# From batch 1 on, x is turned by VectorE block transposes and a trip through DRAM instead of by TensorE

## The chip, the cores and the metric

The program runs on one core of one Trainium2 chip. The time is the device time of one execution in microseconds (us), the median of three runs. Four engines compute: TensorE (PE in the profile; its weight loads are PEld), VectorE (DVE), ScalarE (ACT) and GpSimd (POOL). SyncE (SP) issues all DMAs of this kernel, one after the other in its own program order. Every engine works through its instructions in order, so an instruction that waits holds up all that stand behind it on the same engine.

## The reference

Two stages, in float32, for 8 batches of 576 tokens and 512 channels (8 heads of 64). Attention, of which half the heads see a window of 32 and half a dilated window:

```python
scores = scale * np.matmul(q, k.transpose(0, 1, 3, 2))
scores = np.where(masks[None, :, :, :], scores, -1000000000.0)
attn = softmax over the last axis          # max, exp, sum, divide
x = np.matmul(attn, v), heads side by side # (B, S, 512)
```

and then a mixing stage on its result x:

```python
theta = x @ w_theta
zr, zi = x * np.cos(theta), x * np.sin(theta)
y = einsum('ts,bsd->btd', w_tok_r, zr) + einsum('ts,bsd->btd', w_tok_i, zi)
u = x + y
return u + np.maximum(u @ w_ch, 0.0)
```

## The kernel before

Attention leaves x channel-major: four tiles `xf[b, c]` (c = 0 to 3) with 128 channels on the partitions and 576 tokens along the row. Theta comes out of TensorE the other way, with tokens on the partitions: five tiles, st = 4 (64 tokens) and then st = 0, 1, 2, 3 (128 tokens each), 512 channels along the row. For the products x·cos and x·sin x is therefore needed token-major too. `natural` makes it: for each st, four TensorE transposes (`nc.tensor.transpose` against the identity `idt`, L718) write a 128x512 tile `xn` in PSUM, which the two products read from there.

The work of one tile st after its theta is the trig stage. ScalarE converts theta/2π to an integer (`K`, L746), VectorE takes the fraction (L748), ScalarE makes the sine (`g`, L754), the absolute value (L695) and the cosine (L697), VectorE multiplies by x (L760 sine, L702 cosine; L767 and L702 for the tile of 64), ScalarE rounds the product to `zh` (L641) and GpSimd subtracts to get the rest `zl` (L643). Tiles `K` and `g` have two buffers each.

From batch 1 on the program is a sequence of phases (`phase(b, nb)`), written out in a fixed order. A phase runs the mixing stage of batch b on TensorE while it makes x and z of batch nb = b+1 and begins the attention of batch b+2:

- Eight token units (`token`, L804: 27 matmuls each into a bank `y`), each followed by a residual on VectorE (L782). Between them stand the scores of nb's pairs 2 and 3 and of the next batch's pairs 0 and 1 (L465), and the products with v (`pv`, L614, bank `o`) for the four pairs of nb.
- Scores go through a softmax: the mask and maximum on VectorE (L406, L495), the exponential on ScalarE (L501), the sum's inverse on VectorE (L504, L505), the scaling on GpSimd (L507), and eight 32-row block transposes on VectorE (`turn`, L522) that give `pt`, which `pv` reads.
- After each `pv` ScalarE copies the bank to `x` (L578) and rounds it to `xh` (L590); VectorE subtracts for pairs 0 to 2 (L594, L596), GpSimd for pair 3.
- Then five thetas alternate with channel units (`chan`, L834, 12 matmuls into a bank `c`), each unit followed by a VectorE finish (L813); the `xn` transposes stand in TensorE's order between a channel unit and the next theta. Three channel units close the phase.

Token and channel units share two PSUM banks (tag `m`), so a unit starts only when the residual or finish of the unit two places before it is done. TensorE keeps the order of the code. What VectorE, ScalarE, GpSimd and SP do in a phase is put in order by a scheduler when the program is built. The part up to the end of batch 0 (about the first 142 us) is ordered by `Order` instead, a planner that takes ranks and estimated costs (such as `yield "DVE", 1000`); here the x and z of batch 1 are made. Phases b = 1 to 5 have the same order of VectorE and ScalarE before the change; phase 6 begins no further attention, and phase 7 only mixes.

The changed lines and the functions around them:

Of the kernel before, what the change touches and what calls it, by code (L numbers as in the profile page):

```python
# [48 lines left out]
TURN_AT = {2: 0, 3: 1, 4: 5}  # L49
TURN_TH = {5: 1}  # L50
TH_AT = 7
NK = 9


# [5 lines left out]
class Order:  # L60
# [84 lines left out]
def dma(n):  # L145
    return 128 * 4 * n / 360.0
# [3 lines left out]
def build(ctx, tc, qT, kT, vw, wth, wtk, wch, maskb, ident, identb, outT):  # L150
# [3 lines left out]
    sp = ctx.enter_context(tc.tile_pool(name="soft", bufs=2))  # L154
    xp = ctx.enter_context(tc.tile_pool(name="xu", bufs=2))
    hp = ctx.enter_context(tc.tile_pool(name="hilo", bufs=1))
    gp = ctx.enter_context(tc.tile_pool(name="trig", bufs=2))
    ps_s = ctx.enter_context(tc.tile_pool(name="ps_s", bufs=2, space=PSUM))
    ps_v = ctx.enter_context(tc.tile_pool(name="ps_v", bufs=1, space=PSUM))
# [36 lines left out]
    def give(tag, n):  # L196
        if od.live:
            signal(("free", tag, n))
# [401 lines left out]
    def pv(b, pr):  # L600
        yield None, ("va", b, pr)
        yield None, ("vb", b, pr)
        yield None, ("pt", b, pr)
        if pr >= 1:
            yield None, ("pv", b, pr - 1)
        (va, ra), (vb, rb) = vs["a", b, pr], vs["b", b, pr]
        xf[b, pr] = xp.tile([128, S], F32, tag=f"x{pr}", name=f"x{b}_{pr}")
        n = yield from take("v", 1)
        ps = ps_v.tile([128, 2 * DM], F32, tag="v", name=f"o{b}_{pr}")[:, :S]
        yield "PE", 1300  # L610
        for j in range(NJ):
            v = va[:, j] if j < VA else vb[:, j - VA]
            for hh in range(2):
                pe(nc.tensor.matmul(ps[64 * hh:64 * hh + 64, BW * j:BW * j + BW], v[:, 64 * hh:64 * hh + 64],  # L614
                                    pmats[b, pr][:, j, hh], start=True, stop=True))
        go(x_evac(b, pr, ps, ("v", n), ("xe", b, pr)))
        signal(("pv", b, pr))
        n = b * NP + pr
        if ra is not None:
            give("va", ra)  # L620
            go(load_va(n + 2), RANK["load"])
        if rb is not None:
            give("vb", rb)
            go(load_vb(NP if n == NP - 2 else n + 1), RANK["load"])
        if b:
            go(x_split(b, pr))

    zs = {}

# [63 lines left out]
    def cosine(b, st, f, z, kt, key, rel):  # L693
        yield "ACT", act(DM)
        pin(nc.scalar.activation(f, f, AF.Abs))  # L695
        yield "ACT", act(DM) + 90
        table(nc.scalar.activation(f, f, AF.Sin, scale=-2 * math.pi, bias=halfpi[:f.shape[0]]))  # L697
        signal(("sin", b, st))
        yield None, ("xn", b, st)
        px, rx = pxs[b, st]  # L700
        yield "DVE", dve(DM)
        pin(nc.vector.tensor_tensor(z, px, f, op=ALU.mult))  # L702
        signal(key)
        if kt is not None:
            yield None, ("px", b, st)
            give(*rx)
            yield from zsplit(b, kt, z, rel)
        elif rel:
            give(*rel)

    pxs = {}

    def natural(b, st, cs):
        px, rx = yield from bank("mmxxm"[st] if b == 0 else "x" if b == 1 else XP[st], f"xn{b}_{st}")
        px = px[:cs.stop - cs.start]
        yield "PE", 430
        for c in range(NC):
            pe(nc.tensor.transpose(px[:, 128 * c:128 * c + 128], xf[b, c][:, cs], idt))  # L718
        pxs[b, st] = px, rx
        signal(("xn", b, st))  # L720

    def trig(b, st):
        cs = slice(128 * st, min(128 * st + 128, S))
        R = cs.stop - cs.start
        yield None, ("th", b, st) if b else ("th0", st, 3)
        pt, rt = ths.pop((b, st))
        go(natural(b, st, cs))
        if b == 0 and st in FG0:
            K, gt = (hp.tile([128, DM], F32R, tag=t, name=f"{n}{b}_{st}").bitcast(F32) for t, n in zip(FG0[st], "Kg"))
            K = K.bitcast(I32)[:R]  # L730
            rf = rg = None
        else:
            rf, rg = ("f", (yield from take("f", 2))), ("g", (yield from take("g", 2)))
            K = gp.tile([128, DM], I32, tag="f", name=f"K{b}_{st}")[:R]
            gt = gp.tile([128, DM], F32, tag="g", name=f"g{b}_{st}")
        f = K.bitcast(F32)
        g = gt[:R]
        th = pt[:R]
        if R == 64 and b > 0:
            yield "ACT", act(DM)  # L740
            pin(nc.scalar.copy(g, pt[R:]))
            yield "DVE", dve(DM)
            pin(nc.vector.tensor_tensor(g, th, g, op=ALU.add))
# [10 lines left out]
        table(nc.scalar.activation(g, f, AF.Sin, scale=2 * math.pi))  # L754
        if R == 128:
            go(cosine(b, st, f, f, st, ("cos", b, st), rf))
            yield None, ("xn", b, st)
            px, rx = pxs[b, st]
            yield "DVE", dve(DM)
            pin(nc.vector.tensor_tensor(g, px, g, op=ALU.mult))  # L760
            signal(("px", b, st))
            yield from zsplit(b, 4 + st, g, rg)
        else:
            yield None, ("xn", b, st)
            px, rx = pxs[b, st]
            yield "DVE", dve(DM)
            pin(nc.vector.tensor_tensor(gt[128 - R:], px, g, op=ALU.mult))  # L767
            yield from cosine(b, st, f, g, None, ("cos", b, st), rf)
            give(*rx)
            yield from zsplit(b, 8, gt, rg)  # L770

    uh, ul = {}, {}
# [68 lines left out]
    def phase(b, nb):  # L841
# [5 lines left out]
        while n <= TH_AT:  # L847
            for p in S_AT:
                if S_AT[p] == n and nb + p // NP < B:
                    go(scores(nb + p // NP, p % NP))  # L850
            f, i, g = UNITS[n]
            go(f(b, i, g))
            for p in range(NP):
                if PV_AT[p] == n:
                    go(pv(nb, p))
            for p in TURN_AT:
                if TURN_AT[p] == n and nb + p // NP < B:
                    go(turn(nb + p // NP, p % NP))
            n += 1
        rest = UNITS[n:]  # L860
        for i, st in enumerate(STS):
# [65 lines left out]
    for p in range(2):  # L927
        go(scores(2, p), RANK["scores2"] + p * RANK["pair"])
        go(turn(2, p), RANK["scores2"] + p * RANK["pair"])
    go(thetas(1), RANK["theta1"])  # L930
    od.run()
    od.live = False
# [70 lines left out]
```

## Time and profile before

| | |
|---|---|
| median of three runs | 597.24 us (596.74 to 597.54) |
| the profiled execution | 597.07 us, of which the span from first to last instruction is 595.3 us |
| mean granted TensorE clock | 0.984 |
| busy time in the span | PE 569.7, PEld 516.9, DVE 361.6, ACT 351.1, POOL 222.4 us |
| moved by DMA | 67.76 MB, 114 GB/s on average |

The profile page gives busy times of the engines, the chain of work that ended last, and groups of equal instructions; the trace behind it can be asked for stretches of time, waits, and instructions in order of time. A row of the timeline has the start and the duration in us, the engine, the line, the operation, the tiles (out<-in) and, in brackets, how long the engine stood idle before it and what ended that. A row of the chain of waits has start, duration, engine, tile, line, and how many instructions are merged in it.

### The profile page before, as it was taken

The page shows a single profiled execution, that of the slowest core. Times are in us where ns is not written, and L with a number is a line of the kernel's source. Part 1 is how long each engine was busy: PE and PEld are TensorE (multiplying, and loading weights), DVE is VectorE, ACT ScalarE, POOL GpSimd, SP SyncE. Part 2 cuts the span into 40 slices and gives each one's busy share as a digit, 9 for nine tenths or more (in the row PEclk, how much of TensorE's full clock was granted, in tenths as well). Part 3 has the DMA queues.
Part 4 walks back from the last instruction along what each step waited for, and adds up shares of the span by engine and source line. Part 5 has one row for each costly group of instructions (what it writes and reads, how often), then busy time and mean ns, then how long its engine had stood idle before and what let it go on. Part 6 is the DMA issues. An engine that isn't in the chain of part 4 may idle for free.

```text
span 595.3 us, 14176 instructions
## 1 busy us (share of the span) xinstructions
PE 569.7 (96%) x5584; PEld 516.9 (87%) x5584; DVE 361.6 (61%) x1132; ACT 351.1 (59%) x939; POOL 222.4 (37%) x206
## 2 busy tenths in 40 slices
PE   5997898999999999999999999999999999999997
PEld 4744787979998899889998899989998899989997
DVE  3889888855765667465566567655665656445112
ACT  1498967687535955568553974468564785266110
POOL 2229854534322532326142442316324253315220
PEclk9999599999999999999999999999999999999999
DMA  8982347404650074302641054401742023001002
GB/s 303 398 339 61 121 160 246 142 1 141 182 160 3 2 241 142 101 2 89 197 139 62 1 181 151 154 1 40 231 142 73 0 81 100 1 1 53 28 1 81
DMA packets 26866, 67.76 MB, mean 114 GB/s; under 512 B 2992, under 2 KB 3248, under 8 KB 26800
## 3 DMA queue, kind: packets, MB, share of 16 engines
q1 hardware_dynamic: 26800, 66.86, 32.9%
q8 instruction: 44, 0.72, 0.5%
q14 instruction: 22, 0.18, 0.1%
HBM read 57.41 MB, written 9.44 MB: 112 GB/s over the span
## 4 chain that ended last, share of the span: by engine, by line
PE 49%; DVE 22%; ACT 21%; issue 3%; POOL 2%; DMA 2%; SPq 0%; ACTq 0%; DVEq 0%; POOLq 0%
PE y L804 27%; DVE pt L522 9%; PE c L834 8%; PE s L465 5%; ACT P L501 5%; PE o L614 4%; PE th L682 3%; ACT K L697 3%; ACT zh L641 3%; ACT g L754 2%; ACT K L695 2%; DVE P L406 2%; DVE K L702 2%; POOL P L507 2%; ACT L754 1%
## 5 line engine op out<-in xcount | busy, mean ns | idle before, releaser
L787 POOL TENSOR_TENSOR u<-x,u 128x288 fp32r<-128x288 f32 x64 | 54.9, 858 | 184.9 <-ACT u L785 162.2
L522 DVE STREAM_TRANSPOSE pt<-P 32x288 f32<-32x288 f32 x224 | 105.1, 469 | 21.1 <-POOL P L507 18.0
L834 PE MATMUL c<-u,late_wc 128*128 128x288 f32 x768 | 111.7, 296 | 0.8 <-DVE x L813 0.5
L834 PEld LDWEIGHTS c<-u,late_wc 128*128 128x128 f32 x768 | 106.2, 188 | 4.8 <-DVE x L813 2.0
L785 ACT CAST u<-x 128x288 fp32r<-128x288 f32 x64 | 27.5, 430 | 129.3 <-DVE x L782 129.3
L804 PE MATMUL y<-wtkh,zh 128*128 128x288 f32 x288 | 90.6, 315 | 1.1 <-ACT zh L641 1.1
L804 PE MATMUL y<-wtkh,zl 128*128 128x288 f32 x288 | 86.6, 301 | 3.7 <-POOL zl L643 3.7
L804 PE MATMUL y<-wtkl,zh 128*128 128x288 f32 x288 | 86.2, 299 | 0.0
L643 POOL TENSOR_TENSOR zl<-g,zh 128x512 fp32r<-128x512 f32 x40 | 52.6, 1316 | 79.1 <-ACT zh L641 66.7
L501 ACT ACTIVATE P<-P,mx 128x64 f32<-128x64 f32 x216 | 72.1, 336 | 16.8 <-DVE mx L495 16.8
L682 PE MATMUL th<-wthh,xh 128*128 128x512 f32 x224 | 76.3, 402 | 0.0
L782 DVE TENSOR_TENSOR x<-y,x 128x288 f32<-128x288 f32 x64 | 28.7, 450 | 66.8 <-PE y L804 64.0
L804 PE MATMUL y<-late_wt_b,zh 128*128 128x288 f32 x320 | 68.1, 297 | 0.0
L804 PE MATMUL y<-late_wt_a,zh 128*128 128x288 f32 x256 | 58.0, 308 | 2.7 <-DVE x L782 2.7
L804 PEld LDWEIGHTS y<-wtkh,zh 128*128 128x128 f32 x288 | 55.4, 192 | 4.8 <-ACT zh L641 2.3
L804 PEld LDWEIGHTS y<-wtkh,zl 128*128 128x128 f32 x288 | 55.3, 192 | 4.5 <-POOL zl L643 4.5
L804 PEld LDWEIGHTS y<-wtkl,zh 128*128 128x128 f32 x288 | 55.5, 193 | 0.3 <-issue 0.3
L643 POOL TENSOR_TENSOR zl<-K,zh 128x512 fp32r<-128x512 f32 x32 | 42.0, 1312 | 36.1 <-ACT zh L641 36.1
L507 POOL TENSOR_TENSOR P<-P,sm 128x576 f32<-128x576 f32 x32 | 37.5, 1172 | 43.8 <-ACT xh L590 19.3
L804 PEld LDWEIGHTS y<-late_wt_b,zh 128*128 128x128 f32 x320 | 51.4, 189 | 0.3
L682 PEld LDWEIGHTS th<-wthh,xh 128*128 128x128 f32 x224 | 42.1, 188 | 8.3
L804 PE MATMUL y<-late_wt_b,zl 128*128 128x288 f32 x160 | 47.3, 296 | 0.0
(103 smaller groups left out, 1110.0 us busy)
## 6 DMA issues: line engine op xcount, KB each, us to landing
q<-in_qT_dram SPq DMA_DIRECT2D x32, 576.0 KB, 4.2
va<-in_vw_dram SPq DMA_DIRECT2D x30, 320.0 KB, 3.2
out_dram<-x SPq DMA_DIRECT2D x32, 288.0 KB, 2.1
k<-in_kT_dram SPq DMA_DIRECT2D x28, 304.0 KB, 4.6
vb<-in_vw_dram SPq DMA_DIRECT2D x29, 256.0 KB, 3.4
st_wtk<-in_wtk_dram SPq DMA_DIRECT2D x8, 576.0 KB, 8.8
st_wth<-in_wth_dram SPq DMA_DIRECT2D x4, 512.0 KB, 9.8
st_wch<-in_wch_dram SPq DMA_DIRECT2D x4, 512.0 KB, 4.9
```

Source lines behind the costliest of these rows:

```text
L465: pe(nc.tensor.matmul(ps[64 * e:64 * e + 64, n - g0], q[:, qb], k[:, QB * qb:QB * qb + BW], start=not masked, stop=not masked or n == g1 - 1))
L501: table(nc.scalar.activation(P[:, n], P[:, n], AF.Exp, bias=mx[:, n:n + 1], scale=SCALE, accum_out=sm[:, n:n + 1]))
L507: pin(nc.gpsimd.tensor_tensor(P, P, sm.unsqueeze(2).to_broadcast([128, NJ, BW]), op=ALU.mult))
L522: pin(nc.vector.transpose(pmats[b, pr][k0:k0 + QB, :, hh, QB * e:QB * e + QB], P[p0:p0 + QB, :, QB * o:QB * o + QB]))
L614: pe(nc.tensor.matmul(ps[64 * hh:64 * hh + 64, BW * j:BW * j + BW], v[:, 64 * hh:64 * hh + 64], pmats[b, pr][:, j, hh], start=True, stop=T ...
L643: pin(nc.gpsimd.tensor_tensor(lo, z, hi.bitcast(F32), op=ALU.subtract))
L682: pe(nc.tensor.matmul(pt, l, r, start=(n == 0), stop=(n == 3 * NC - 1)))
L782: pin(nc.vector.tensor_tensor(x[:, ts], ps, x[:, ts], op=ALU.add))
L785: pin(nc.scalar.copy(uh[b, d][:, ts], x[:, ts]))
L787: pin(nc.gpsimd.tensor_tensor(ul[b, d][:, ts], x[:, ts], uh[b, d][:, ts].bitcast(F32), op=ALU.subtract))
L804: pe(nc.tensor.matmul(ps, l[:, cs], r, start=(n == 0), stop=(n == 3 * NK - 1)))
L834: pe(nc.tensor.matmul(ps, l[:, cs], r[:, ts], start=(n == 0), stop=(n == 3 * NC - 1)))
```

## The change

For batch 0 nothing changes. From batch 1 on:

- `natural` returns at once: the 20 TensorE transposes of a batch and their PSUM tiles are gone.
- `x_turn`: after each pair's x is in SBUF, one VectorE block transpose on 128 rows writes it, 32x32 block by block, into `xq` (128 x 18 x 32 elements each, four of them a batch).
- `x_store`: after the fourth, four DMAs, one for each 32 partitions of `xq`, write 288 KB each to a scratch `xd` in DRAM, in runs of 512 bytes.
- `x_load`: five DMAs bring `xd` back as `xn`, now token-major in SBUF, 128 KB for the tile of 64 tokens and 256 KB for each of the others. They wait for the stores. `xq` and `xn` share one SBUF buffer in turn.
- `by_x`: the products read `xn` from SBUF, with columns grouped by another order, and so have two inputs in SBUF.

```diff
+LOAD_AT = 6
...
             go(x_split(b, pr))
+            go(x_turn(b, pr))
+            if pr == NP - 1:
+                go(x_store(b))
...
-        px, rx = pxs[b, st]
         yield "DVE", dve(DM)
-        pin(nc.vector.tensor_tensor(z, px, f, op=ALU.mult))
+        by_x(b, st, z, f)
...
+    def x_turn(b, c):
+        yield None, ("xe", b, c)
+        if c == 0:
+            xq[b] = cp.tile([128, 5 * DM], F32, tag="xn", name=f"xq{b}")[:, :NC * S]
+            xq[b] = xq[b].rearrange("p (a c s) -> p a c s", c=NC, s=QB)
...
+        yield "DVE", 1000
+        pin(nc.vector.transpose(xq[b][:, :, c], xf[b, c].rearrange("p (a s) -> p a s", s=QB)))
...
+    def x_store(b):
...
+        rows_of = dp.tile([S, DM], F32, tag="xd", name=f"xd{b}")
+        to = rows_of.rearrange("(a s) (g f) -> s a g f", s=QB, g=4)
+        yield "DMA", dma(NC * S)
+        for g in range(4):
+            pin(nc.sync.dma_start(to[:, :, g], xq[b][QB * g:QB * g + QB].rearrange("p a c s -> p a (c s)")))
...
+    def x_load(b):
+        yield None, ("xd", b)
+        rows_of = xds[b]
+        xn = cp.tile([128, 5 * DM], F32, tag="xn", name=f"xn{b}").rearrange("p (a d) -> p a d", d=DM)
+        for st in STS:
+            R = 64 if st == 4 else 128
+            yield "DMA", dma(DM)
+            pin(nc.sync.dma_start(xn[:R, st], rows_of[128 * st:128 * st + R]))
...
     def natural(b, st, cs):
-        px, rx = yield from bank("mmxxm"[st] if b == 0 else "x" if b == 1 else XP[st], f"xn{b}_{st}")
+        if b:
+            return
+        px, rx = yield from bank("mmxxm"[st], f"xn{b}_{st}")
...
+    def by_x(b, st, z, f):
+        if b:
+            pin(nc.vector.tensor_tensor(rows(z), xns[b, st], rows(f), op=ALU.mult))
+        else:
+            pin(nc.vector.tensor_tensor(z, pxs[b, st][0], f, op=ALU.mult))
...
+            if n == LOAD_AT:
+                go(x_load(nb))
...
+    go(x_load(1), 0)
     go(thetas(1), RANK["theta1"])
...
-    nc = _bacc.Bacc("TRN2", target_bir_lowering=False, num_devices=1)
+    nc = _bacc.Bacc("TRN2", target_bir_lowering=False, num_devices=1,
+                     dynamic_dma_scratch_size=1024)
```

Lines shift: of what the prediction speaks of, L406 becomes L408, L522 L524, L596 L598, L641 L646, L643 L648, L748 L802, L782 L835, L813 L866; the products are all L772 and the new transposes L730.

VectorE's order in phase 3 (x of batch 4 is made), between the softmax of pair 3 and the residual `x_3`. In a tile's name the number behind it is the pair, the channel tile or st. Before:

```order
L495 TENSOR_SCALAR mx_3_3645<-mx_3_3645 128x9
L782 TENSOR_TENSOR x_2_2913<-y_2_0_3762,x_2_2913 128x288
L504 TENSOR_SCALAR sm_3_3646<-sm_3_3646 128x9
L505 RECIPROCAL sm_3_3646<-sm_3_3646 128x9
L594 TENSOR_TENSOR xh_1_3750<-x_1_3725,xh_1_3750 128x64
L596 TENSOR_TENSOR xh_1_3750<-x_1_3725,xh_1_3750 128x512
L522 STREAM_TRANSPOSE pt_107<-P_3_3644 32x9x32 x8
L594 TENSOR_TENSOR xh_2_3819<-x_2_3794,xh_2_3819 128x64
L596 TENSOR_TENSOR xh_2_3819<-x_2_3794,xh_2_3819 128x512
L782 TENSOR_TENSOR x_3_3054<-y_3_0_3823,x_3_3054 128x288
```

VectorE at the same place after:

```order
L497 TENSOR_SCALAR mx_3_3622<-mx_3_3622 128x9
L730 STREAM_TRANSPOSE xq_3611<-x_1_3702 128x18x32
L835 TENSOR_TENSOR x_2_2900<-y_2_0_3740,x_2_2900 128x288
L506 TENSOR_SCALAR sm_3_3623<-sm_3_3623 128x9
L507 RECIPROCAL sm_3_3623<-sm_3_3623 128x9
L596 TENSOR_TENSOR xh_1_3727<-x_1_3702,xh_1_3727 128x64
L598 TENSOR_TENSOR xh_1_3727<-x_1_3702,xh_1_3727 128x512
L730 STREAM_TRANSPOSE xq_3611<-x_2_3772 128x18x32
L524 STREAM_TRANSPOSE pt_109<-P_3_3621 32x9x32 x8
L596 TENSOR_TENSOR xh_2_3797<-x_2_3772,xh_2_3797 128x64
L598 TENSOR_TENSOR xh_2_3797<-x_2_3772,xh_2_3797 128x512
L835 TENSOR_TENSOR x_3_3042<-y_3_0_3802,x_3_3042 128x288
```

The transpose of x_1 stands ahead of the residual `x_2`, that of x_2 ahead of the turn of pair 3. The other two stand behind L507 of pair 2, ahead of the masks of pair 3 (x_0), and behind L507 of the next batch's pair 0, ahead of its turn (x_3).

VectorE's order in the trig stage of the same phase, from tile 1's fraction on (`c_2_0` to `c_1_1` are the channel units 2 to 5). Before:

```order
L748 SCALAR_TENSOR_TENSOR K_1_4246<-th_1_4214,K_1_4246 128x512
L813 SCALAR_TENSOR_TENSOR x_2_2913<-c_2_0_4227,x_2_2913 128x288
L702 TENSOR_TENSOR K_1_4246<-xn_1_4241,K_1_4246 128x512
L760 TENSOR_TENSOR g_1_4247<-xn_1_4241,g_1_4247 128x512
L748 SCALAR_TENSOR_TENSOR K_2_4295<-th_2_4263,K_2_4295 128x512
L813 SCALAR_TENSOR_TENSOR x_3_3054<-c_3_0_4276,x_3_3054 128x288
L702 TENSOR_TENSOR K_2_4295<-xn_2_4290,K_2_4295 128x512
L760 TENSOR_TENSOR g_2_4296<-xn_2_4290,g_2_4296 128x512
L748 SCALAR_TENSOR_TENSOR K_3_4345<-th_3_4312,K_3_4345 128x512
L813 SCALAR_TENSOR_TENSOR x_0_2726<-c_0_1_4325,x_0_2726 128x288
L813 SCALAR_TENSOR_TENSOR x_1_2844<-c_1_1_4362,x_1_2844 128x288
```

VectorE there after:

```order
L802 SCALAR_TENSOR_TENSOR K_1_4222<-th_1_4195,K_1_4222 128x512
L866 SCALAR_TENSOR_TENSOR x_2_2900<-c_2_0_4208,x_2_2900 128x288
L772 TENSOR_TENSOR K_0_4170<-xn_4068,K_0_4170 128x512
L772 TENSOR_TENSOR g_1_4223<-xn_4068,g_1_4223 128x512
L772 TENSOR_TENSOR K_1_4222<-xn_4068,K_1_4222 128x512
L866 SCALAR_TENSOR_TENSOR x_3_3042<-c_3_0_4252,x_3_3042 128x288
L802 SCALAR_TENSOR_TENSOR K_2_4266<-th_2_4239,K_2_4266 128x512
L772 TENSOR_TENSOR g_2_4267<-xn_4068,g_2_4267 128x512
L802 SCALAR_TENSOR_TENSOR K_3_4311<-th_3_4283,K_3_4311 128x512
L772 TENSOR_TENSOR K_2_4266<-xn_4068,K_2_4266 128x512
L866 SCALAR_TENSOR_TENSOR x_0_2710<-c_0_1_4296,x_0_2710 128x288
L772 TENSOR_TENSOR g_3_4312<-xn_4068,g_3_4312 128x512
```

Channel unit 4's finish (`c_0_1`) now stands behind the cosine product of tile 2, and that of unit 5 behind the sine product of tile 3; before, both stood right behind the fraction of tile 3.

SP's order in the same phase, at the end of the loads. Before:

```order
L231 DMA va_1_3956<-in_vw_dram 128x640
L247 DMA vb_0_3958<-in_vw_dram 128x512
L218 DMA q_3_4035<-in_qT_dram 128x1152
L220 DMA k_3_4036<-in_kT_dram 128x608
L819 DMA out_dram<-x_0_2726 128x576
```

SP there after:

```order
L233 DMA va_1_3935<-in_vw_dram 128x640
L249 DMA vb_0_3937<-in_vw_dram 128x512
L741 DMA xd_3944<-xq_3611 32x18x128 x4
L220 DMA q_3_4020<-in_qT_dram 128x1152
L222 DMA k_3_4021<-in_kT_dram 128x608
L752 DMA xn_4068<-xd_3944 64x512
L752 DMA xn_4068<-xd_3944 128x512 x4
L872 DMA out_dram<-x_0_2710 128x576
```

The four stores stand ahead of the load of the next q and k, the five loads behind it and ahead of the outputs.

More of the change, by code (lines that the diff above doesn't have):

```diff
@@ L156, in build @@
     hp = ctx.enter_context(tc.tile_pool(name="hilo", bufs=1))
+    dp = ctx.enter_context(tc.tile_pool(name="dram", bufs=2, space=bass.MemoryType.DRAM))
     gp = ctx.enter_context(tc.tile_pool(name="trig", bufs=2))
@@ L699, in cosine @@
         yield None, ("xn", b, st)
-        px, rx = pxs[b, st]
         yield "DVE", dve(DM)
-        pin(nc.vector.tensor_tensor(z, px, f, op=ALU.mult))
+        by_x(b, st, z, f)
         signal(key)
         if kt is not None:
-            yield None, ("px", b, st)
-            give(*rx)
+            if not b:
+                yield None, ("px", b, st)
+                give(*pxs[b, st][1])
             yield from zsplit(b, kt, z, rel)
@@ L757, in trig @@
             yield None, ("xn", b, st)
-            px, rx = pxs[b, st]
             yield "DVE", dve(DM)
-            pin(nc.vector.tensor_tensor(g, px, g, op=ALU.mult))
+            by_x(b, st, g, g)
             signal(("px", b, st))
@@ L764, in trig @@
             yield None, ("xn", b, st)
-            px, rx = pxs[b, st]
             yield "DVE", dve(DM)
-            pin(nc.vector.tensor_tensor(gt[128 - R:], px, g, op=ALU.mult))
+            by_x(b, st, gt[128 - R:], g)
             yield from cosine(b, st, f, g, None, ("cos", b, st), rf)
-            give(*rx)
+            if not b:
+                give(*pxs[b, st][1])
             yield from zsplit(b, 8, gt, rg)
```

12 lines of the change are left out of this document (added).

## The prediction

> **What bounds the kernel now.** I read the page's engine totals first, then the windows of one steady phase and of phase 6, then what TensorE waits for, then the chain of waits.
>
> TensorE is busy nearly all the time. The rows of the windows give the stretch, its length, and busy time (count of instructions) of PE, PEld, DVE, ACT and POOL, then granted clock, DMA share and GB/s; the first row is the end of the live part, the second a steady phase (b = 3), the third phase 6.
>
> ```profile
> PE 569.7 (96%) x5584; PEld 516.9 (87%) x5584; DVE 361.6 (61%) x1132; ACT 351.1 (59%) x939; POOL 222.4 (37%) x206
> ```
>
> ```profile
> 120.00:142.30 22.30, 21.27 (x127) 18.87 (x125) 12.31 (x20) 18.37 (x30) 9.46 (x8) 1.00 0.08 29
> 276.20:344.90 68.70, 67.91 (x677) 63.07 (x677) 42.73 (x155) 42.23 (x121) 24.38 (x24) 1.00 0.32 106
> 482.50:550.30 67.80, 67.80 (x629) 64.09 (x630) 34.22 (x100) 39.14 (x89) 25.03 (x25) 1.00 0.14 49
> ```
>
> In phase 6 TensorE does nothing but work: 67.80 of 67.80. In the steady phase 67.91 of 68.70 are filled, and the waits there (for whom: total, times, longest) are small:
>
> ```profile
> PE y L804 <- DVE x L782: 0.5, 1, 0.5
> PE c L834 <- DVE x L813: 0.2, 1, 0.2
> ```
>
> This alone reads as a kernel bound by TensorE, which would profit from 20 groups of transposes less. The chain (start, duration, engine, tile, line) reads otherwise:
>
> ```profile
> 142.41 1.20 PE s L465 x36
> ...
> 279.69 1.20 PE s L465 x36
> ...
> 311.76 3.78 PE y L804 x27
> 315.55 0.45 DVE x L782
> ...
> 321.85 1.17 POOL P L507
> ...
> 326.92 0.69 DVE g L743
> ...
> 341.83 0.73 ACT K L697
> 342.59 0.69 DVE K L702
> 343.28 0.60 DVE g L760
> ...
> 344.47 0.38 DVE x L813
> ...
> 344.89 3.46 PE c L834 x24
> 348.35 1.20 PE s L465 x36
> ...
> 526.01 0.44 PE xn L718 x4
> ...
> 545.10 0.44 PE xn L718 x4
> ```
>
> From 279.69 to 348.35 (one phase, 68.66) TensorE carries the chain up to 315.55. From there it runs over VectorE's masks, the exponentials, GpSimd's scaling (321.85), the turn, the theta step g (326.92) and the trig stage, and comes back to TensorE at 344.89 behind the finish at 344.47. No `xn` stands in it. Only phase 6 has them, five of 0.44 (first and last shown). Two chains of nearly the same length compete, then: TensorE's own, and the one over VectorE and ScalarE, which is the longer by some tenths. Shortening the first gives nothing while the second stands; lengthening the second costs its full amount.
>
> **The change part by part.** I go by three parts of a steady phase: scores to g (279.69 to 326.92, 47.23), g to the finish of channel unit 4 (to 344.47, 17.55), and from there to the next scores (3.88).
>
> *Removed: the xn transposes.* Form by form (count | total, mean ns):
>
> ```profile
> L718 PE MATMUL xn<-idt,x 128*128 128x128 f32 x128 | 19.8, 278 | 2.9 <-DVE g L702 1.5 <-DVE K L702 1.1
> L522 DVE STREAM_TRANSPOSE pt<-P 32x288 f32<-32x288 f32 x224 | 105.1, 469 | 21.1 <-POOL P L507 18.0
> ```
>
> On TensorE it is 5 x 0.44 = 2.2 a phase by the chain's rows. In phases 1 to 5 that is worth 0; it becomes idle time ahead of channel units. In phase 6 it lies on the chain: -2.2. But pair 3 there also waits for a turn that is one new transpose (0.4 of which show) later: -1.8.
>
> *Added: four transposes of 128x576 on VectorE.* Rows of VectorE, and behind them of ScalarE, from the places where they will stand (start, duration, line, tiles, size; in brackets idle time before it):
>
> ```profile
> 286.50 0.22 DVE L406 CUSTOM_DVE_ANT_0 P<-s,mskb 128x64 f32<-128x64 f32 x1 [0.84 <-PE s L465]
> ...
> 295.70 0.46 DVE L782 TENSOR_TENSOR x<-y,x 128x288 f32<-128x288 f32 x1 [2.40 <-PE y L804]
> ...
> 297.95 1.65 DVE L596 TENSOR_TENSOR xh<-x,xh 128x512 fp32r<-128x512 f32 x1
> ...
> 303.56 0.69 DVE L596 TENSOR_TENSOR xh<-x,xh 128x512 fp32r<-128x512 f32 x1
> ...
> 311.66 3.85 DVE L522 STREAM_TRANSPOSE pt<-P 32x288 f32<-32x288 f32 x8 [1.90 <-POOL P L507]
> ...
> 334.45 0.69 DVE L702 TENSOR_TENSOR K<-xn,K 128x512 f32<-128x512 f32 x1 [1.64 <-ACT K L697]
> ```
>
> ```profile
> 285.92 0.64 ACT L578 COPY x<-o 128x576 f32<-128x576 f32 x1 [0.29 <-PE o L614]
> ...
> 294.12 0.35 ACT L501 ACTIVATE P<-P,mx 128x64 f32<-128x64 f32 x1
> ...
> 309.53 1.19 ACT L578 COPY x<-o 128x576 f32<-128x576 f32 x1
> ...
> 335.18 0.63 ACT L641 CAST zh<-K 128x512 fp32r<-128x512 f32 x1 [0.28 <-DVE K L702]
> ```
>
> No row shows a block transpose on 128 partitions; a 32x288 takes 0.469. Lower bound: like that one, 0.47. Upper bound: each quarter of the partitions by itself, 4 x 0.78 = 3.1. In between, 128-row instructions take 0.46 for 288 elements (L782) and 0.69 for 512 (L702), about 1.05 ns an element, whatever the partitions hold; so I take the partitions as free, 0.30 of the 0.469 as streaming and 0.17 as fixed, and get 0.17 + 2 x 0.30 = 0.77, near the lower bound since every row here streams by elements of a row. One by one:
>
> - x_0: its copy ends at 285.92 + 0.64 = 286.56, the transpose at 287.33 and, with a gap, the masks at about 287.35: they started at 286.50 before, so +0.86. They lead to the exponentials at 294.12. Those had stood behind the copy of x_1 (like that of x_0, 0.64), which ScalarE now makes ahead of a cast that waits, so part is given back; I take +0.4 (bounds 0.2 and 0.9).
> - x_1: ahead of residual 2, where VectorE idles 2.40 (row 295.70): 0. Without that idle, 0.77.
> - x_2: between L596 at 297.95 and the turn, where VectorE has no gap: +0.78.
> - x_3: its copy ends at 310.72, the transpose at 311.49, and the turn at 311.66 waited 1.90 for GpSimd: 0, with 0.2 to spare; without the cover up to 0.6.
>
> From 303.56 on masks, exponentials, scaling and turns follow on one another, so all of it reaches g. First part: +1.2.
>
> *Moved: the products read SBUF twice.* Rows of GpSimd:
>
> ```profile
> 143.05 1.28 POOL L643 TENSOR_TENSOR zl<-K,zh 128x512 fp32r<-128x512 f32 x1
> ...
> 299.01 1.26 POOL L787 TENSOR_TENSOR u<-x,u 128x288 fp32r<-128x288 f32 x1
> ...
> 305.21 0.80 POOL L787 TENSOR_TENSOR u<-x,u 128x288 fp32r<-128x288 f32 x1 [4.95 <-ACT u L785]
> ...
> 333.87 1.29 POOL L643 TENSOR_TENSOR zl<-g,zh 128x512 fp32r<-128x512 f32 x1 [10.11 <-ACT zh L641]
> ```
>
> L596, whose inputs both lie in SBUF, took 0.69 alone (303.56) and 1.65 at 297.95 while GpSimd worked; GpSimd's cast residue took 0.80 alone and 1.26 then. The product at 334.45 has one input in PSUM, ran inside `zl` (333.87 to 335.16), and took 0.69. So a product from SBUF costs nothing alone and up to 0.96 more beside `zl`. [...]
>
> In the new order of the trig stage, for the second part: the cosine product of tile 1 runs into a `zl` (+0.8), ScalarE converts tile 3 ahead of the cosine of tile 2 (+0.6); the three waits of ScalarE for a product (0.28 at 335.18), two of them in this stretch, go (-0.55); and between that cosine and the finish of unit 4 stands one product instead of product, product and fraction (344.47 - 342.59 = 1.88 becomes 0.7, with rounding -1.1). These nearly cancel, -0.25; as the fit of several queues is never perfect I take 0 (bounds -0.8, nothing blocked, and +1.0, one more blocked). Third part: the finish of unit 5 stands behind the sine product of tile 3, which takes up to 1.3 beside a `zl`. Unit 6 (half of 3.46) covers most of finish 4, product and finish 5 (0.4 + 1.3 + 0.5, and 0.1 for a later sine); unit 7 starts 0 to 0.6 late, and I take 0.28. A phase: 1.2 + 0 + 0.28 = 1.5, and five: +7.4.
>
> *Added: four stores, five loads.*
>
> ```profile
> q1 hardware_dynamic: 26800, 66.86, 32.9%
> ```
>
> ```profile
> out_dram<-x SPq DMA_DIRECT2D x32, 288.0 KB, 2.1
> ```
>
> A store of 288 KB lands in 2.1 (`out_dram`); if the queues took all four together it would be 2.1, and 2.1 again for the first load: 4.2 in all, the lower bound. Upper bound by packets: 32.9% of 16 engines x 595.3 over 26800 is 0.117 us a packet, and 1.18 MB in runs of 512 bytes is 2304 packets: 2304 x 0.117 / 16 = 16.8. With 2.5 for the first load 19.3. I take 6 + 2.5 = 8.5, nearer to the lower end, since the 2.1 is measured on a store of that size and the packets' mean holds far larger ones. In a steady phase x_3 is turned at about 312.7 and tile 4's sine product comes 3.9 after g, at 332: 19 us of cover, so 0 (at the upper bound 0.3). SP holds back the next q and k by the wait for x_3 and four issues, and the outputs behind the loads; q and k of pair 3 are first read more than 30 later: 0.
>
> In the live part VectorE has the least room:
>
> ```profile
> 118.88 0.68 DVE L743 TENSOR_TENSOR g<-th,g 64x512 f32<-64x512 f32 x1
> ...
> 122.21 0.68 DVE L767 TENSOR_TENSOR g<-xn,g 64x512 f32<-64x512 f32 x1 [1.26 <-ACT g L754]
> ```
>
> It works nearly without gaps up to 118.88, so four transposes are 3.1 late, while g stands two steps of the turn (2 x 0.48) earlier: 121.0. x_3 is ready by 120.0, the first load by 128.5, so the product at 122.21 is 6.3 late. ScalarE has 22.30 - 18.37 = 3.9 of idle time to catch up; the last `zl` (143.05 + 1.28 = 144.33) is read by the seventh ninth of the first token unit, 143.6 + 6/9 x 3.78 = 146.1, room of 1.8. That leaves 6.3 - 3.9 - 1.8 = 0.6, and with one product blocked behind `zl` (0.7) +1.3. Bounds: -2.2 (the transposes gone, nothing late) and +12.1 (transfer 19.3).
>
> Sum against the profiled run, 597.07 (span 595.3 and 1.77 around it; the median is 0.17 more): 597.07 + 7.4 + 1.3 - 1.8 = 604.0.
>
> **The rivals.**
>
> *TensorE is the bound after all (faster).* For it: 96% busy, waits of 0.7 a phase, `xn` on phase 6's chain. Against: none in five phases. It decides if the first part's +1.2 were hidden and the trig stage's shorter way to finish 4 (the -1.1 and -0.55, without the +0.8) made the second chain over 1.5 shorter. Then seven batches give 7 x 2.2 = 15.4, 581.7 at most; half of it, 589.4, is likelier, since that chain is only tenths apart.
>
> *No change.* The products don't block. Then the second part is -0.8, the third 0, a phase +0.4: 597.07 + 2 + 1.3 - 1.8 = 598.6; with x_0's transpose hidden too, 596.6. For it: 334.45 ran unharmed. Against: that one read PSUM, and L596 did not.
>
> *Late transfers.* With stores at 10 to 16.8 us the first load lands after 12.5 to 19.3, and the live part grows one for one, +4 to +10.8: 608 to 615. At the upper end each phase pays 0.3 too: 616. The packet row speaks for it; against it stands the 2.1 of a store of equal size.
>
> *Transposes quarter by quarter.* 3.1 each: x_0 and x_2 2.3 more each, x_1 and x_3 partly exposed, about +8 a phase: 645. For it: rows of L522 show only 32 partitions. [...]
>
> **How the numbers follow.** About 0.2% (1.2 us) is what the measurement can tell from no change. Forecast 0.55 (598.5 to 610, a phase from +0.4 with nothing blocked to +2.7 with every product blocked, by the bounds above); late transfers 0.15; quarter by quarter 0.04; no change 0.10; TensorE bound 0.16. Faster 0.16, same 0.10, slower 0.74. The range leaves out the farther half of the faster case (0.08), 645 (0.04) and the end of the late transfers and of blocked products (0.06): 592 to 616.
>
> **What would show it.** Right: L730 at about 0.77 and L772 at a mean well above 0.69, GpSimd's L648 above 1.3; TensorE's busy time down by 35 x 0.44 = 15; a phase of about 70.1; more waits of `c` for the finish (L866) in each phase; phase 6 shorter by 1 to 2; stores landing within 10. Wrong: a phase under 68 with no new wait on L866; L772 at 0.69 throughout; a live part that ends more than 5 later; L730 over 1.

## The result, and the profile after

| | before | after |
|---|---|---|
| median of four runs, same chip | 596.99 us (596.69 to 597.54) | 612.63 us (611.98 to 612.97) |
| ratio | | 1.026 (95%: 1.0242 to 1.0277) |
| span of the profiled execution | 595.3 us | 611.2 us |
| mean granted TensorE clock | 0.984 | 0.975 |

The change costs 15.6 us. The forecast was 604.0: the direction was right, the amount less than half of what came. (Lines have shifted by the change: in the rows below L467 is the scores, L857 the token units, L887 the channel units and L866 their finish. In the kernels of the experiments the same lines move by a few more.)

The engine totals of the page after, to be held against those of before:

```profile
PE 562.9 (92%) x5444; PEld 508.6 (83%) x5444; DVE 404.9 (66%) x1160; ACT 348.4 (57%) x939; POOL 229.0 (37%) x206
```

TensorE works 6.8 us less, VectorE 43.3 more. Twenty-eight new transposes are 21.6 of VectorE's growth (the groups by form below: count | total, mean ns | idle time before them). The products have become slower as well, 1.14 and 1.00 in the mean where those from PSUM took 0.69:

```profile
L730 DVE STREAM_TRANSPOSE xq<-x 128x576 f32<-128x576 f32 x28 | 21.6, 772 | 10.7 <-ACT x L580 10.6
L772 DVE TENSOR_TENSOR g<-xn,g 128x512 f32<-128x512 f32 x28 | 31.8, 1136 | 6.9 <-ACT g L808 6.5 <-DMA xn<-xd 0.3
L772 DVE TENSOR_TENSOR K<-xn,K 128x512 f32<-128x512 f32 x28 | 27.9, 995 | 6.0 <-ACT K L702 5.5
```

Where the time went shows when the scores that open each phase are put side by side. (The live part is the stretch ahead of phase 1, which the planner `Order` puts in order.) The chain of waits of after (start, duration, engine, tile, line, count), answering to 142.41, 279.69 and 348.35 of before:

```profile
147.74 0.76 PE s L467 x20
...
226.08 1.20 PE s L467 x36
...
296.27 1.20 PE s L467 x36
...
365.04 1.20 PE s L467 x36
...
433.84 1.20 PE s L467 x36
...
504.03 1.20 PE s L467 x36
```

and the same for the phases of before that have not been shown:

```profile
211.01 1.20 PE s L465 x36
...
417.24 1.20 PE s L465 x36
...
485.93 1.20 PE s L465 x36
```

| stretch | before | after | difference |
|---|---|---|---|
| live part and phase 1 (to 211.01, 226.08) | 211.01 | 226.08 | +15.07 |
| phase 2 | 68.68 | 70.19 | +1.51 |
| phase 3 | 68.66 | 68.77 | +0.11 |
| phase 4 | 68.89 | 68.80 | -0.09 |
| phase 5 | 68.69 | 70.19 | +1.50 |
| phases 6 and 7 (to the end of the span) | 109.37 | 107.17 | -2.20 |

The sum is +15.9, the difference of the two spans. Nearly all of it has arisen before phase 1 is half done: the third scores of that phase start 15.12 later (this is called the live loss below), and from there on the rest of the phase takes as long as before. The same instruction in the timelines of TensorE, before and after:

```profile
163.30 1.27 PE L465 MATMUL s<-k,q 128*64 128x64 f32 x36
```

```profile
178.42 1.27 PE L467 MATMUL s<-k,q 128*64 128x64 f32 x36
```

Two of the steady phases cost 1.5, which is the number that the forecast had for each of them; two cost nothing. That the number fits those two is luck, and the experiments ask what sets them apart.

What the live part looks like after, in its chain of waits:

```profile
123.20 5.54 DMA xd<-xq
...
129.36 2.96 DMA xn<-xd
...
132.41 0.70 DVE g L772
...
138.17 4.61 PE th L687 x12
142.78 1.59 PE c L887 x12
144.37 2.97 PE th L687 x12
...
148.90 0.61 DVE K L802
...
152.11 1.28 ACT L503
...
153.41 2.76 ACT P L503 x16
156.17 0.52 ACT zh L646
...
156.75 1.27 POOL zl L648
...
158.07 2.05 PE y L857 x7
```

Two things are to be seen. The products wait for the trip: the fourth transpose ends at 121.03, the stores have landed at 128.74, and the chain's product runs at 132.41 (the first one at 131.38, behind 2.73 us in which VectorE waited for the load; before it ran at 122.21). And the order of the instructions is another: the fraction of theta 3 (148.90) stands behind the first masks of phase 1's scores, and on ScalarE a table load and eight exponentials (152.11 to 156.17, 4.06 us) stand ahead of the rounding of the last product, `zh`, for which the first token unit waits.

### The profile page after: what moved, and what is told of

Read it like the earlier page. It is cut to its first block, busy times and chain, and to the rows that moved or that the text cites. A ratio compares the mean times of both kernels' runs of the same rounds, so it can differ in the third digit from the quotient of the medians.

```text
span 611.2 us, 13968 instructions
## 1 busy us (share of the span) xinstructions
PE 562.9 (92%) x5444; PEld 508.6 (83%) x5444; DVE 404.9 (66%) x1160; ACT 348.4 (57%) x939; POOL 229.0 (37%) x206
## 4 chain that ended last, share of the span: by engine, by line
PE 32%; DVE 29%; ACT 21%; POOL 8%; issue 5%; DMA 3%; SPq 1%; ACTq 0%; DVEq 0%; POOLq 0%
PE y L857 15%; DVE pt L524 13%; ACT P L503 8%; PE c L887 8%; POOL zl L648 5%; DVE P L408 3%; PE th L687 3%; DVE xh L598 2%; PE o L616 2%; PE s L467 2%; POOL P L509 2%; ACT K L800 2%; ACT K L702 2%; ACT g L808 2%; DVE xq L730 2%
## 5 line engine op out<-in xcount | busy, mean ns | idle before, releaser
L887 PE MATMUL c<-u,late_wc 128*128 128x288 f32 x768 | 113.6, 302 | 15.7 <-DVE x L866 14.1
L887 PEld LDWEIGHTS c<-u,late_wc 128*128 128x128 f32 x768 | 109.1, 193 | 21.0 <-DVE x L866 16.2
L524 DVE STREAM_TRANSPOSE pt<-P 32x288 f32<-32x288 f32 x224 | 104.9, 468 | 13.8 <-POOL P L509 8.5
L857 PE MATMUL y<-wtkh,zh 128*128 128x288 f32 x288 | 91.0, 316 | 7.0 <-ACT zh L646 6.9
L648 POOL TENSOR_TENSOR zl<-g,zh 128x512 fp32r<-128x512 f32 x40 | 56.6, 1419 | 101.4 <-ACT zh L646 88.4
L857 PE MATMUL y<-wtkh,zl 128*128 128x288 f32 x288 | 87.1, 303 | 4.5 <-POOL zl L648 4.5
L857 PE MATMUL y<-wtkl,zh 128*128 128x288 f32 x288 | 86.5, 300 | 0.0
L503 ACT ACTIVATE P<-P,mx 128x64 f32<-128x64 f32 x216 | 72.1, 335 | 15.9 <-DVE mx L497 15.6
L857 PE MATMUL y<-late_wt_b,zh 128*128 128x288 f32 x320 | 68.8, 299 | 0.0
L857 PEld LDWEIGHTS y<-wtkh,zh 128*128 128x128 f32 x288 | 55.7, 194 | 10.7 <-ACT zh L646 8.3
L835 DVE TENSOR_TENSOR x<-y,x 128x288 f32<-128x288 f32 x64 | 28.7, 450 | 54.0 <-PE y L857 53.6
L857 PE MATMUL y<-late_wt_a,zh 128*128 128x288 f32 x256 | 57.7, 307 | 4.3 <-DVE x L835 4.3
L857 PEld LDWEIGHTS y<-wtkh,zl 128*128 128x128 f32 x288 | 55.7, 193 | 5.5 <-POOL zl L648 5.5
L857 PEld LDWEIGHTS y<-wtkl,zh 128*128 128x128 f32 x288 | 55.9, 194 | 0.3 <-issue 0.3
L857 PEld LDWEIGHTS y<-late_wt_b,zh 128*128 128x128 f32 x320 | 51.7, 190 | 0.3
L648 POOL TENSOR_TENSOR zl<-K,zh 128x512 fp32r<-128x512 f32 x32 | 45.5, 1421 | 12.6 <-ACT zh L646 12.3
L857 PE MATMUL y<-late_wt_b,zl 128*128 128x288 f32 x160 | 47.5, 297 | 0.0
```

The source lines that it names most:

```text
L503: table(nc.scalar.activation(P[:, n], P[:, n], AF.Exp, bias=mx[:, n:n + 1], scale=SCALE, accum_out=sm[:, n:n + 1]))
L524: pin(nc.vector.transpose(pmats[b, pr][k0:k0 + QB, :, hh, QB * e:QB * e + QB], P[p0:p0 + QB, :, QB * o:QB * o + QB]))
L648: pin(nc.gpsimd.tensor_tensor(lo, z, hi.bitcast(F32), op=ALU.subtract))
L835: pin(nc.vector.tensor_tensor(x[:, ts], ps, x[:, ts], op=ALU.add))
L857: pe(nc.tensor.matmul(ps, l[:, cs], r, start=(n == 0), stop=(n == 3 * NK - 1)))
L887: pe(nc.tensor.matmul(ps, l[:, cs], r[:, ts], start=(n == 0), stop=(n == 3 * NC - 1)))
```

## The experiments

Two theories stood at the start: that the data come late (A), and that the order which the planner of the live part makes, or the transposes themselves, carry the loss (B). The first four kernels ran on one chip, where the kernel before had a median of 597.96 us (23 runs, 595.69 to 599.2).

**Data early, order kept (early1).**

```diff
+        if b == 1 and c == 3:
+            flat = qT[1, 0].rearrange("p a c -> (p a c)")[:128 * DM].rearrange("(p d) -> p d", d=DM)
+            for st in STS:
+                R = 64 if st == 4 else 128
+                pin(nc.sync.dma_start(xn1[0][:R, st], flat[:R]))
...
-        for g in range(4):
+        for g in range(4 if b > 1 else 0):
```

(For batch 1 the stores are left out and the loads bring a part of q. `xn1` takes the place of the loads' tile, and the transposes of batch 1 write one small tile in turn.)

> The order of PE, VectorE, ScalarE and GpSimd stays that of the changed kernel. For batch 1 alone the stores are left out and the five loads bring other data of the same size (a part of q), at the same place of SP's order, so they no longer wait for the fourth transpose and the stores; the transposes of batch 1 still run. Batches 2 to 7 as in the changed kernel (the output of batch 1 is not the reference's). Theory A (the trip through DRAM comes 9.2 us late in the live part, 131.38 instead of 122.21, and that is where the +15.1 us up to the scores S0 of phase 1 start): the first product comes at about 125, the live loss falls from 15.1 to 2 to 5, the time to 599 to 603. Theory B (the planner's order of the live part and the transposes on VectorE carry it, the wait hides in them): 608 or more. The prediction's own term (+1.3 there, +7.4 in the phases) would give 611 to 613, no change.

Measured: 609.35 us (605.98 to 609.61), ratio 1.0181 (1.0151 to 1.0211). The third scores of phase 1 stand at 175.12, where on this chip they stand at 164.1 to 164.2 with the live part of before (the two kernels below): a loss of 11.0 instead of 15.1. Theory A fails as the main cause: with the data there in time, nearly three quarters of the loss remain. The first product does not run when its sine is ready (126.23 + 0.63 = 126.86, a row of ScalarE) but at 130.09, because VectorE's order puts it behind the fraction of the next tile, for which VectorE waits 2.44:

```profile
126.23 0.63 ACT L822 ACTIVATE g<-K 64x512 f32<-64x512 f32 x1
```

```profile
129.00 0.69 DVE L816 SCALAR_TENSOR_TENSOR K<-th,K 128x512 f32<-128x512 f32 x1 [2.44 <-ACT K L814]
...
130.09 1.41 DVE L786 TENSOR_TENSOR g<-xn,g 64x512 f32<-64x512 f32 x2
```

The chain of this run has the same 4.06 us on ScalarE ahead of the last `zh`:

```profile
148.99 1.28 ACT L503
...
150.29 2.76 ACT P L503 x16
153.05 0.52 ACT zh L646
```

**The transposes left out as well (early1_noturn).** As early1, with

```diff
-        if b == 1:
-            pin(nc.vector.transpose(xq[b]..., xf[b, c]...))
-        else:
+        if b > 1:
             pin(nc.vector.transpose(xq[b][:, :, c], ...))
```

> As early1, and the four VectorE transposes of batch 1 are left out too, with the rest of the order unchanged (output of batch 1 not the reference's). What remains of the live loss is then the order alone and products that read SBUF beside GpSimd. Theory A: 3.1 us less on VectorE before the theta step, of which 2 to 3 show: 597 to 600. Theory B with the order alone: within 1 us of early1. If the transposes are the main cost: 6 or more below early1.

Measured: 609.21 us (606.51 to 610.69), ratio 1.0192 (1.0164 to 1.0219), in the medians no different from early1, as theory B expected; the runs of both kernels spread over some 4 us. In the profile the third scores are at 173.73, 1.4 earlier than in early1, but that is not the transposes: this execution was ahead already before the first of them would stand. A mask matmul that both have in common (`s<-mskb`) starts at 81.35 here and at 83.25 in early1, with a granted clock of 1.00 against 0.76 from 69 to 78. Counted from there the two differ by 0.5, the other way. So no price of the four transposes in the live part can be read from this pair; it is small. The order is left as the main part.

**Batch 1 by TensorE, the others by the new way (b2_on).**

```diff
+TRIP = (2, 3, 4, 5, 6, 7)
...
-        if b:
+        if b in TRIP:
             pin(nc.vector.tensor_tensor(rows(z), xns[b, st], rows(f), op=ALU.mult))
```

> Only batches 2 to 7 take the new way, batch 1 keeps TensorE's transposes and the planner its old order of the live part. Theory A: the live part is again that of before (scores of phase 1 at 142.4); a steady phase costs 0 to 0.2 where TensorE's clock stays at 1.00 and 1.5 where it falls, phase 6 saves 2.2: 595 (no fall) to 600 (three falls or more). The prediction's sum for the phases (+1.5 each in four or five, -1.8) would give 601 to 603.

Measured: 598.52 us (595.51 to 599.99), ratio 1.001 (0.9992 to 1.0029): no difference from before. So batches 2 to 7 together cost nothing that can be measured, and the live part carries the change's loss. In the profiled run four phases last 68.8 and one 70.4. The chain has the same 24 matmuls at the end of an undisturbed and of the long phase, and the windows (columns as in the prediction) give their clock:

```profile
345.96 3.54 PE c L889 x24
...
414.94 4.99 PE c L889 x24
```

```profile
408.00:413.00 5.00, 4.92 (x32) 4.39 (x30) 4.21 (x5) 3.96 (x7) 4.55 (x3) 1.00 0.00 0
413.00:419.80 6.80, 4.86 (x24) 4.75 (x24) 5.15 (x8) 4.73 (x9) 4.22 (x3) 0.75 0.35 133
```

In the last window the granted clock is 0.75, and units that take 3.54 take 4.99. The 1.5 of the long phases are that (the long one here is phase 4, which before was 0.2 longer than the others as well, 68.89).

**Batch 7 alone (b7_only).** `TRIP = (7,)`, so only phase 6 changes.

> Only batch 7, which is made in phase 6, takes the new way. Phase 6 is the one phase where TensorE is busy without a gap and the xn transposes stand on the chain. Theory A: 2.2 us less than before (five groups of 0.44), 594.8, faster than both kernels. Rival (what phase 6 saved in the changed kernel was recovered time of its late start): 596.5 to 597.5.

Measured: 595.91 us (594.24 to 596.95), ratio 0.9969 (0.9957 to 0.9982). Phases 6 and 7 take 594.2 - 486.84 = 107.4 instead of 109.4. This is the version that beats both kernels, by 2.0 us, in the one phase in which TensorE has no gap (64.20 busy of 64.20 from 486.8 to 551 in this run, 67.80 of 67.80 in phase 6 before).

```profile
486.84 1.20 PE s L468 x36
```

**Order and wait taken apart (plan_early, both_early).** Early1 keeps an order that was made for late data, because the planner counts the trip (3.3 us for the stores, 0.7 for a load, 1.8 for each landing). In the next two kernels it counts nothing for batch 1:

```diff
-        yield "DMA", dma(NC * S)
+        if b > 1:
+            yield "DMA", dma(NC * S)
...
-            yield "DMA", dma(DM)
+            if b > 1:
+                yield "DMA", dma(DM)
```

plan_early has this alone, both_early this and the edits of early1. The kernel before had a median of 597.17 (13 runs, 595.79 to 599.6) on this chip.

> The changed kernel, but the planner that orders the live part takes stores and loads of batch 1 as free of cost; the transfers themselves stay as they are. So the order of the engines becomes one made for early data (theta 3 ahead of three channel units again, the cast of the last zh ahead of the exponentials), and the data come as late as before. Theory C (after early1: the order, made for late data, carries about 10 of the 15 us, the wait itself the rest): the live loss is what the lateness alone costs, 4 to 7, and the time 601 to 606. Theory D (order and wait are one thing, the late product holds up any order): live loss 12 or more, 609 to 613.

> As early1 (batch 1 loads other data of the same size, no stores, its output not the reference's), and ordered as in plan_early. Wait and late order are both gone; what is left of the live loss is four transposes and products from SBUF. Theories C and D: live loss 2 to 4, 597 to 602. If the transposes or the products beside GpSimd were the cause: still 8 or more lost, 605 to 609.

Measured: plan_early 608.74 us (607.85 to 610.06), ratio 1.0195 (1.0165 to 1.0226); both_early 602.11 (601.32 to 603.04), ratio 1.0083 (1.0056 to 1.011). With the third scores of phase 1 as the measure (164.6 and 165.1 with the live part of before on this chip, 164.8 taken) the four cases are:

| live loss, us | data late | data early |
|---|---|---|
| order made for late data | 15.1 (after) | 11.0 (early1) |
| order made for early data | 9.2 (plan_early) | 3.3 (both_early) |

The order costs 5.9 to 7.7, the wait 4.1 to 5.9, whichever of the two is taken away first, and 3.3 remain for the transposes, the products from SBUF and the rest, which were not taken apart. Each cell rests on one profile, and executions differ before the live part's new work begins: counted from the mask matmul named above (81.35 to 83.80 in these profiles) the four cells are 14.2, 10.8, 8.9 and 4.1. That makes the order 5.3 to 6.7 and the wait 3.4 to 4.8, so the split is known to about 1 us, and the order is at least as large a part as the wait by either count. Neither theory of plan_early was right in its numbers: 9.2 lies between the 4 to 7 of the one and the 12 of the other. In both_early the last `zh` stands ahead of the table load again:

```profile
148.32 0.62 ACT zh L646
...
148.96 1.28 ACT L503
```

**TensorE's gaps filled (b2_fill), and transposes without a reader (b2_dead).** Both from b2_on, on the chip of the last two:

```diff
     def natural(b, st, cs):
-        if b in TRIP:
-            return
...
     def by_x(b, st, z, f):
-        if b in TRIP:
+        if False:
```

The first edit, the transposes into PSUM for every batch, is b2_fill; with the second too, products from there, it is b2_dead.

> b2_on with the xn transposes of TensorE kept for all batches, into PSUM where nothing reads them; the products still read SBUF. TensorE's idle 2 us ahead of channel unit 6 are filled again. Theory E (TensorE's clock falls after the new idle time, and that is all a steady phase of 70.2 has over one of 68.8): no phase with a clock below 1.00 for the last units, all steady phases 68.7 to 69.0, phase 6 saves nothing: 597 to 599. Rival (units slowed by the transfers or by something else than idle time): phases of 70.2 as often as in b2_on, one or two in five.

> As b2_fill, but the products read the PSUM tiles as in the kernel before, while transposes, stores and loads still run with nobody reading the result. This has the transposes' price alone, without products that meet GpSimd. Prediction's terms: first part of a phase +1.2 by the transposes, so 69.9 a phase, 603 in all. Theory F (the first part's growth is mostly given back ahead of the trig stage): at most 69.2 a phase, 597 to 600; and against b2_fill the difference is the price of the blocked products, which the prediction put at 1.1 a phase.

Measured: b2_fill 602.82 us (602.61 to 603.15), ratio 1.0093 (1.0063 to 1.0123); b2_dead 601.47 (598.89 to 602.36), ratio 1.0064 (1.0046 to 1.0082). Two consecutive scores in the chains of b2_fill and b2_dead:

```profile
282.97 1.20 PE s L468 x36
...
352.60 1.20 PE s L468 x36
```

```profile
282.96 1.20 PE s L468 x36
...
352.34 1.20 PE s L468 x36
```

All ten steady phases of the two runs last 69.4 to 69.9, and in none does the clock fall at the end. With the gap there are 11 falls in 32 phases (those of after, early1, early1_noturn, plan_early, both_early, b2_on and cost1 in which the last 24 matmuls run on behind a wait of 2.0 to 2.2). Without it there are none in 25: the ten here, and the fifteen of before, b7_only and b1_only. The theory of the clock agrees; the sizes were expected wrong (597 to 599 for b2_fill). b2_dead's 69.38 a phase and 601.47 in all lie between its two theories (69.9 and 603; at most 69.2 and 600).

Read as a sum, a steady phase is 68.66 before; 69.38 with the transposes and a trip that nobody reads, +0.72; 69.63 with products from SBUF too, +0.25; 68.77 without TensorE's transposes (b2_on), -0.86. The +0.1 of the undisturbed phases is made of these three. Only a part of this is a clean price. The stretch from the scores to g, 47.23 before, is 47.8 in all of b2_dead, b2_fill, b2_on and after, so the new transposes cost 0.56 there. Behind g the scheduler has ordered VectorE anew in each kernel, and a step holds its share of that, too.

**The live part alone (b1_only), and a planner that is told the right time (cost1).** `TRIP = (1,)`, and in the changed kernel

```diff
-        yield "DMA", dma(NC * S)
+        yield "DMA", 6500
```

> Only batch 1, which is made in the live part, takes the new way; batches 2 to 7 keep TensorE's transposes. If the live part alone carries the change's loss, the scores S0 of phase 1 come 14 to 16 us later than before, all later phases are as before (68.6 to 68.9 each, no fall of the clock), and the time is 611 to 613, no less than the whole change. By the prediction's terms (+1.3 live) it would be 598 to 599.

> The changed kernel, with the planner told 6.5 us instead of 3.3 for the four stores of each batch, so that its first load lands about when it does on the chip (some 11 us after the last transpose). Theory C (the loss comes from the order together with the wait; an order made for later data puts still more channel units and scores ahead of thetas): live loss 14 to 20, 611 to 617. Theory G (the loss comes from the planner's error of some 3 us, so that a right figure heals it): live loss below 8, under 606.

Measured, with 598.12 us for the kernel before on this chip (7 runs, 596.83 to 598.81): b1_only 610.65 (610.03 to 611.01), ratio 1.021 (1.0193 to 1.0228); cost1 609.77 (607.4 to 610.09), ratio 1.0185 (1.0156 to 1.0214). b1_only is 12.5 above before, somewhat less than expected; all its steady phases last 68.7. The batch of the live part alone costs four fifths of the change. cost1 is a miss for both sides: the planner's error of 3 us is not the matter, but the later estimate did not make the order worse either (third scores at 176.75, after 178.42). What helped was the order that the planner makes when it is told of no trip at all (plan_early), though the data came just as late.

## Why the prediction was wrong, step by step

- **The live part: +1.3, measured +15.1.** This is the step that failed. The prediction let a product that is 6.3 late be caught up by ScalarE's idle time (3.9) and by the room ahead of the last `zl` (1.8). The product came 9.2 late (131.38 against 122.21). The transfer was too short in the sum: 8.5 to the first product's data, against 131.38 - 121.03 = 10.35, most of it in the stores (121.03 to 128.74, 7.7 where 6 was taken; the first load with 2.6 was near the 2.5 taken). But that is the smaller fault: with 9.2 the same sum gives 9.2 - 3.9 - 1.8 + 0.7 = 4.2, still 10.9 short. The larger fault was to keep the order of before in that sum. The planner makes the live part's order from its own estimate of the trip, and with late products the rest of the trig stage is placed late: masks ahead of the last fraction, a table load and eight exponentials ahead of the last `zh`. Idle time of ScalarE was no use to work that stood behind other work. The experiments put 5 to 8 us on that order and 3 to 6 on the wait. The bound above, +12.1, was too low for the same reason. (A live part that ends more than 5 later was among the prediction's own signs of being wrong.)
- **The rival of late transfers: the right time by the wrong way.** Its 608 to 615 hold the 612.6 that came, but its condition did not: the stores landed after 7.7, not after 10 to 16.8, and with the wait taken away 11.0 of the loss stayed (early1).
- **The steady phases: +1.5 each, measured +0.1, and +1.5 where the clock fell.** In phase 3 the first part grew by 0.56 (296.27 to 344.06, against 47.23): of the two terms, x_2's came (+0.7), x_0's +0.4 did not, since the masks lost some 0.8 but the exponentials of pair 3, with the copy of x_1 moved ahead of the cast, began 14.3 after the scores where they had begun 14.4 after them. The second part was 0.6 shorter (344.06 to 360.98, against 17.55) where 0 was taken, and the third +0.2 where +0.28 was.

```profile
344.06 0.69 DVE g L797
...
360.98 0.46 DVE x L866
...
361.48 3.56 PE c L887 x24
```

- **TensorE's transposes in the steady phases: 0, measured -0.86** (b2_fill to b2_on). The rival of TensorE as the bound may have that much right, but it is not shown: no `xn` stands in b2_fill's chain either, all of the 0.86 lies behind g, and there VectorE's order is another in the two kernels. By which path it comes is open. TensorE's busy time fell by 6.8 where 15 was forecast; its mean clock fell as well, 0.984 to 0.975, and at a lower clock the same matmuls are busy for longer (24 of them 4.99 at 0.72, 3.56 at 1.00).
- **The products beside GpSimd: right in kind.** Products from SBUF took 1.70 and 1.61 where they met a `zl`, and the `zl` 1.64 instead of 1.30 (VectorE, then GpSimd, of phase 3):

```profile
352.59 0.68 DVE L772 TENSOR_TENSOR K<-xn,K 128x512 f32<-128x512 f32 x1
353.27 1.70 DVE L772 TENSOR_TENSOR g<-xn,g 128x512 f32<-128x512 f32 x1
355.07 1.61 DVE L772 TENSOR_TENSOR K<-xn,K 128x512 f32<-128x512 f32 x1
```

```profile
351.17 1.30 POOL L648 TENSOR_TENSOR zl<-g,zh 128x512 fp32r<-128x512 f32 x1 [10.27 <-ACT zh L646]
352.79 1.64 POOL L648 TENSOR_TENSOR zl<-g,zh 128x512 fp32r<-128x512 f32 x1 [0.31 <-ACT zh L646]
```

  The price of the two side by side was put too high: 0.25 a phase by the difference of b2_fill and b2_dead, with the two orders' share in it, not 1.1.
- **The transposes' own price: right.** 0.772 in the mean on 128 partitions; the forecast's 0.77 was the author's estimate from rows of 32, and the 3.1 of the rival quarter by quarter did not come. **Phase 6: right.** -2.2, forecast -1.8, and b7_only shows it alone. **The transfers in steady phases: right**, hidden; the only products that waited for a load are those at 131.38 and 132.41, in the live part.

That 612.63 still lies in the range is luck and no merit of the sum: the steady phases were put 4.4 too high (+7.4 for five, against 1.51 + 0.11 - 0.09 + 1.50 = 3.0 for phases 2 to 5 and 0 for the rest of phase 1; and even these 3.0 are the clock's) and the live part 13.8 too low.

## What to carry to other kernels

Where a planner or scheduler makes the order from estimated times, a new latency acts twice, as a wait and through the order that is made around it; here the order was worth 5 to 8 us and the wait 3 to 6, and removing either alone left most of the loss. Read the order after for what stands between the late data and its last reader, on every engine on the way, before any idle time is counted as room. And put a change that relieves an engine where that engine has no gap: in phase 6 alone it gave 2.0 us, in the other phases nothing, and in the part with the least room it cost 12.5.

## What the hardware showed that was not expected

TensorE's granted clock fell after new idle time (to 0.72 in two phases of four), and not each time. In each of phases 2 to 5 after, TensorE waits 2.0 us for the finish of channel unit 4 (waits of phase 3):

```profile
PE c L887 <- DVE x L866: 2.0, 1, 2.0
```

In phases 3 and 4 the clock stays at 1.00 all the same; in phases 2 and 5 it is 0.72 for the 6 us that follow, and 24 matmuls take 4.99 instead of 3.56:

```profile
290.00:296.20 6.20, 4.92 (x25) 4.75 (x25) 4.38 (x7) 4.12 (x9) 4.21 (x3) 0.72 0.37 143
358.00:365.00 7.00, 4.96 (x37) 4.50 (x36) 6.05 (x8) 5.47 (x10) 5.18 (x4) 1.00 0.25 96
```

With the gap filled by transposes that nobody reads (b2_fill), or by those that the products read (b2_dead), none of ten phases had such a fall. Waits of the same 2.0 us stand ahead of the phase ends with a fall and of those without; what decides between two equal waits no run here shows. In the live part the clock falls as well: it is 0.64 from 138.1 to 142.8, where theta 2 takes 4.61 (138.17), and 1.00 from 142.8 to 147.4, where theta 3 takes 2.97 (144.37). No run takes that apart, but the granted clock of the windows bounds it. From 116 us to the third scores it is 1.00 before, and:

| | stretch | length | granted clock | the clock's share at most |
|---|---|---|---|---|
| after | 116 to 178.4 | 62.4 | 0.92 | 5.0 |
| early1 | 116 to 175.1 | 59.1 | 0.94 | 3.5 |
| plan_early | 116 to 174.0 | 58.0 | 0.94 | 3.5 |
| both_early | 116 to 168.1 | 52.1 | 0.97 | 1.6 |

The last column is an estimate, the length times what the clock lacks of 1.00; it is less where TensorE had nothing to do at the time. With all of it taken off, the four cells of the live loss are 10.1, 7.5, 5.7 and 1.7, and the order is still 4.4 to 5.8 and the wait 2.6 to 4.0. So the clock can explain only a part of either.
